# Q's last 64 contraction rows as two 64-row array tiles in an attention kernel

## The chip, the cores and the metric

The kernel runs on one core of one Trainium2 chip. The metric is device microseconds (us) of one execution. A kernel is timed in several runs and its median is quoted. Engines are named as in the profile: PE is TensorE's matmul, PEld its weight load (which normally overlaps PE), DVE is VectorE, ACT is ScalarE, POOL is GpSimd, SPq is the queue that issues DMA.

## The reference

Two independent attention blocks, A and B, have the same shapes; their outputs are concatenated. All data is bf16.

```python
B, Sq, D = 16, 144, 448            # x: [B, Sq, D]
H, Sk, Dh = 16, 512, 256           # k_cache, v_cache: [B, H, Sk, Dh]
q = (x @ wq).reshape(B, Sq, H, Dh).transpose(0, 2, 1, 3)
scores = einsum("bhqd,bhkd->bhqk", q, k_cache) * Dh ** -0.5
p = softmax(scores)
o = einsum("bhqk,bhkd->bhqd", p, v_cache)
out = o.transpose(0, 2, 1, 3).reshape(B, Sq, H * Dh) @ wo
```

What matters: Q contracts over D = 448 = 3 x 128 + 64, so the last of its four chunks fills only half of the 128 rows of TensorE's array.

## The kernel before

A unit is one head of one batch; there are 512. For each unit the kernel computes Q (transposed, 256 rows in two halves `dc` of 128), the scores S against K, exp, PV, and the output projection OP. Q is computed either for one batch (80 groups, 144 columns a matmul) or, in most of the kernel, for one head of a pair of batches (216 groups, 288 columns a matmul). The last 64 rows of Wq sit on partitions 64 to 127 of chunk 3, and partitions 0 to 63 of that chunk are set to zero once. So every matmul uses all 128 rows.

```python
wq_sb = sb("wq_sb", [128, 4, H * DH], BF16)
qp_ps = ps("qp_ps", [128, 2, 512], F32)            # two PSUM banks
# ... (cut)
def e2(v):
    return v.memset(wq_sb[0:64, 3, :], 0.0)        # zero rows of the last chunk
# ... (cut) Wq arrives by groups of four heads:
q.dma_start(wq_sb[:, 0:3, cols], w[0:384, cols].rearrange("(c p) n -> p c n", p=128))
q.dma_start(wq_sb[64:128, 3, cols], w[384:448, cols])
# ... (cut)
def t_q(U):                                        # n = 1 or 2 batches
    def e(t):
        for dc in range(2):
            for kc in range(4):
                c0 = h * DH + dc * 128
                acc = qp_ps[:, dc, 0:2 * SQ] if n == 2 else qp_ps[:, 0, dc * SQ:(dc + 1) * SQ]
                ins = t.matmul(acc, lhsT=wq_sb[:, kc, c0:c0 + 128],
                               rhs=xt_sb[:, kc, xo:xe + 1:max(xe - xo, 1), :], start=(kc == 0), stop=(kc == 3))
        return ins
```

A helper builds the order of the instructions on each engine; DVE copies the result of each group out of PSUM (`qt_sb<-qp_ps`).

## Time and profile before

| | before |
|---|---|
| median of the first 3 runs | 1057.1 us (1055.59 to 1058.32) |
| span of the profiled run | 1055.3 us |
| PE busy | 1031.0 us, 98% |
| DVE / ACT / POOL busy | 70% / 75% / 60% |
| Q groups | 80 of one batch, 216 of two |

The first part of the profile's page gives the busy time of each engine, its share of the span, and its instructions; the fourth part, the shares of the chain of waits that ended last:

```profile
PE 1031.0 (98%) x12376; PEld 875.0 (83%) x12376; DVE 740.9 (70%) x2039; ACT 793.9 (75%) x2365; POOL 636.6 (60%) x1030
...
PE 91%; DMA 5%; ACT 1%; DVE 1%; SPq 1%; issue 0%; POOL 0%; ACTq 0%; DVEq 0%
```

PE is the bottleneck. A busy PE need not stream at its best rate, so the next view matters more. This is the timeline of PE from 397 us: start in us, duration, engine, line, operation, output and inputs, rows and columns of the weights (`128*128`), the shape of the input, and how many matmuls the line merges.

```profile
397.78 0.54 PE L1259 MATMUL op_ps<-wo_sb,ring 128*128 128x448 bf16 x2
398.16 1.14 PE L1052 MATMUL qp_ps<-xt_sb,wq_sb 128*128 128x288 bf16 x8
399.14 0.66 PE L1086 MATMUL s_ps<-qt_sb,kt_sb 128*128 128x144 bf16 x8
399.64 0.66 PE L1142 MATMUL ot_ps<-pt_sb,v_sb 128*128 128x144 bf16 x8
400.14 0.54 PE L1259 MATMUL op_ps<-wo_sb,ring 128*128 128x448 bf16 x2
```

Read the starts, not the durations (one matmul's recorded duration overlaps the next). The eight matmuls of a pair's Q group take 399.14 - 398.16 = 0.98 us, 122.5 ns each for 288 columns; eight of 144 columns take 0.50 us, 62.5 ns each. The difference is 60 ns for 144 columns, so a column costs 0.417 ns and each matmul about 2.5 ns more. There is nothing between the groups: in this stretch PE streams columns without a gap, and as long as it does, only fewer columns can make it faster.

What PE waited for, in us in total, times, and the longest:

```profile
PE s_ps L1000 <- DMA v_sb<-in_A_k_cache_dram: 6.3, 4, 4.7
PE qp_ps L1052 <- DMA wq_sb<-in_B_wq_dram: 3.6, 1, 3.6
PE s_ps L1086 <- DMA kt_sb<-in_B_k_cache_dram: 2.9, 1, 2.9
PE qp_ps L1052 <- DMA xt_sb<-in_A_x_dram: 2.3, 1, 2.3
```

### The profile page before, as it was taken

What the parts mean: (1) busy time and instruction counts of PE and PEld (TensorE: products, weight loads), DVE (VectorE), ACT (ScalarE), POOL (GpSimd) and SP (SyncE); (2) the same over time, 40 slices, a digit from 0 to 9 for tenths busy, and PEclk for the clock granted to TensorE, in tenths of its full rate; (3) what the DMA queues carried; (4) which work ended last, traced back from release to release, by engine and by line L of the source; (5) the groups of instructions that cost most, each with busy time, mean ns of one, the idle gap of its engine ahead of it and who ended that gap; (6) DMA issues with size and microseconds to landing.
All of it is one profiled execution on the core that took longest, in us unless ns stands there. A gap on an engine that the chain in (4) does not pass through costs nothing.

```text
span 1055.3 us, 32320 instructions
## 1 busy us (share of the span) xinstructions
PE 1031.0 (98%) x12376; PEld 875.0 (83%) x12376; DVE 740.9 (70%) x2039; ACT 793.9 (75%) x2365; POOL 636.6 (60%) x1030
## 2 busy tenths in 40 slices
PE   6999999999999999999999899999999999999997
PEld 6999888888888888888878788888888888888885
DVE  4776666776766777777868667677776667777775
ACT  4887667777777777878857667777877777788785
POOL 3554556656666566666746556566666666666673
PEclk9999999999999999999999999999999999999999
DMA  9999999999999999999999999999999999999960
GB/s 316 372 343 291 294 291 248 283 299 271 264 305 260 248 286 262 304 289 280 283 281 343 279 283 287 303 284 292 251 279 280 278 286 298 296 254 274 292 201 14
DMA packets 589060, 294.15 MB, mean 279 GB/s; under 512 B 500832, under 2 KB 513632, under 8 KB 588896
## 3 DMA queue, kind: packets, MB, share of 16 engines
q1 hardware_dynamic: 588896, 291.99, 110.9%
q8 instruction: 99, 1.62, 0.6%
q14 instruction: 65, 0.53, 0.2%
HBM read 161.48 MB, written 4.13 MB: 157 GB/s over the span
## 4 chain that ended last, share of the span: by engine, by line
PE 91%; DMA 5%; ACT 1%; DVE 1%; SPq 1%; issue 0%; POOL 0%; ACTq 0%; DVEq 0%
PE s_ps L1086 23%; PE ot_ps L1142 23%; PE qp_ps L1052 22%; PE op_ps L1259 19%; DMA kt_sb<-in_B_k_cache_dram 2%; DMA v_sb<-in_A_k_cache_dram 2%; PE ot_ps L1158 2%; PE s_ps L1000 1%; PE qp_ps L1000 1%; DMA wq_sb<-in_B_wq_dram 1%; PE qp_ps L1259 1%; ACT rinv_sb L1179 0%; ACT pt_sb L1096 0%; DVE ring L1194 0%; DVE qt_sb L1066 0%
## 5 line engine op out<-in xcount | busy, mean ns | idle before, releaser
L1106 POOL TENSOR_TENSOR pp_sb<-pt_sb 128x288 f32<-128x288 bf16 x512 | 384.9, 752 | 322.5 <-ACT pt_sb L1096 308.1
L1096 ACT ACTIVATE pt_sb<-s_ps 128x288 bf16<-128x288 f32 x1024 | 364.6, 408 | 184.4 <-PE s_ps L1086 177.6
L1194 DVE TENSOR_TENSOR ring<-ot_ps,rinv_sb 128x288 bf16<-128x288 f32 (+2 forms) x640 | 241.9, 394 | 150.3 <-ACT rinv_sb L1179 145.8
L1086 PE MATMUL s_ps<-qt_sb,kt_sb 128*128 128x144 bf16 x4096 | 341.3, 226 | 4.7 <-DMA kt_sb<-in_B_k_cache_dram 2.9
L1142 PE MATMUL ot_ps<-pt_sb,v_sb 128*128 128x144 bf16 x4096 | 340.3, 226 | 0.0
L1086 PEld LDWEIGHTS s_ps<-qt_sb,kt_sb 128*128 128x128 bf16 x4096 | 287.7, 98 | 56.9 <-DVE qt_sb L1066 5.6
L1179 ACT ACTIVATE rinv_sb<-ln_sb 64x144 f32<-64x144 f32 x928 | 298.3, 321 | 24.3
L1052 PE MATMUL qp_ps<-xt_sb,wq_sb 128*128 128x288 bf16 (+1 forms) x2368 | 302.3, 271 | 6.6 <-DMA wq_sb<-in_B_wq_dram 3.6
L1259 PE MATMUL op_ps<-wo_sb,ring 128*128 128x448 bf16 x1120 | 285.2, 353 | 0.0
L1052 PEld LDWEIGHTS qp_ps<-xt_sb,wq_sb 128*128 128x128 bf16 x2368 | 212.3, 98 | 81.9 <-issue 7.5
L1142 PEld LDWEIGHTS ot_ps<-pt_sb,v_sb 128*128 128x128 bf16 x4096 | 274.5, 98 | 0.5
L1111 POOL TENSOR_TENSOR p_sb<-pp_sb 128x144 f32<-128x144 f32 x464 | 227.5, 490 | 74.6 <-DVE ps_sb L1120 10.4
L1209 DVE TENSOR_REDUCE run_sb<-ot_ps 128x1 bf16<-128x144 f32 x560 | 146.5, 304 | 79.4 <-ACT ln_sb L1166 44.3
L1120 DVE TENSOR_TENSOR ps_sb<-p_sb 64x144 bf16<-64x144 f32 x464 | 158.7, 342 | 44.4 <-POOL p_sb L1111 30.3
L1066 DVE CAST qt_sb<-qp_ps 128x576 bf16<-128x576 f32 x216 | 162.1, 751 | 21.3 <-PE qp_ps L1052 17.7
L1259 PEld LDWEIGHTS op_ps<-wo_sb,ring 128*128 128x128 bf16 x1120 | 94.0, 98 | 21.2
L1166 ACT ACTIVATE ln_sb<-ot_ps 128x144 f32<-128x144 f32 x232 | 67.9, 293 | 32.6 <-PE ot_ps L1158 25.3
L1158 PE MATMUL ot_ps<-ps_sb,ones 128*128 128x144 bf16 x280 | 63.4, 226 | 0.0
L1065 DVE CAST qt_sb<-qp_ps 128x288 bf16<-128x288 f32 x80 | 35.9, 448 | 4.8 <-PE qp_ps L1052 4.3
L1008 ACT ACTIVATE kt_sb<-qp_ps 128x512 bf16<-128x512 bf16 x48 | 28.9, 603 | 7.3 <-PE qp_ps L1000 7.3
L1111 POOL TENSOR_TENSOR ps_sb<-pp_sb 128x144 bf16<-128x144 f32 x48 | 23.5, 490 | 6.9 <-PE ot_ps L1158 0.3
L1158 PEld LDWEIGHTS ot_ps<-ps_sb,ones 128*128 128x128 bf16 x280 | 27.5, 98 | 0.0
(29 smaller groups left out, 153.4 us busy)
## 6 DMA issues: line engine op xcount, KB each, us to landing
v_sb<-in_A_v_cache_dram SPq DMA_DIRECT2D x128, 512.0 KB, 7.1
v_sb<-in_B_v_cache_dram SPq DMA_DIRECT2D x128, 512.0 KB, 7.5
v_sb<-in_A_k_cache_dram SPq DMA_DIRECT2D x24, 512.0 KB, 9.6
out_dram<-ost_sb SPq DMA_DIRECT2D x36, 112.0 KB, 6.2
wo_sb<-in_A_wo_dram SPq DMA_DIRECT2D x8, 448.0 KB, 8.7
wo_sb<-in_B_wo_dram SPq DMA_DIRECT2D x8, 448.0 KB, 9.0
wq_sb<-in_A_wq_dram SPq DMA_DIRECT2D x4, 768.0 KB, 10.1
wq_sb<-in_B_wq_dram SPq DMA_DIRECT2D x4, 768.0 KB, 10.6
```

What stands on the lines that cost most here:

```text
L1052: ins = t.matmul(acc, lhsT=wq_sb[:, kc, c0:c0 + 128], rhs=xt_sb[:, kc, xo:xe + 1:max(xe - xo, 1), :], start=(kc == 0), stop=(kc == 3))
L1066: return v.tensor_copy(qt_sb[:, a:b + 1:b - a, :, :], qp_ps[:, :, 0:2 * SQ].rearrange("p e (u q) -> p u e q", u=2))
L1086: ins = t.matmul(s_ps[bank][:, (c % 2) * SQ:(c % 2 + 1) * SQ], lhsT=kt_sb[:, 2 * c + dc, ko:ko + 128], rhs=qt_sb[:, qsl, dc, :], start=(dc ...
L1096: return a.activation(pt_sb[:, psl, 2 * k:2 * k + 2, :].rearrange("p b q -> p (b q)"), s_ps[bank][:, 0:2 * SQ], AF.Exp, scale=DH ** -0.5)
L1106: return g.tensor_tensor(pp_sb[:, :, :], pt_sb[:, psl, 0:2, :], pt_sb[:, psl, 2:4, :], op=ALU.add)
L1111: return g.tensor_tensor(dst, pp_sb[:, 0, :], pp_sb[:, 1, :], op=ALU.add)
L1120: return v.tensor_tensor(ps_sb[p0:p0 + 64, sl, :], p2_sb[0:64, :], p2_sb[64:128, :], op=ALU.add)
L1142: ins = t.matmul(ot_ps[ob][:, dc * SQ:(dc + 1) * SQ], lhsT=v_sb[:, vsl, j, c * DH + dc * 128:c * DH + (dc + 1) * 128], rhs=pt_sb[:, sl, c, ...
L1179: return a.activation(rinv_sb[p0:p0 + 64, sl, :], ln_sb[h0:h0 + 64, :], AF.Exp, scale=-1.0)
L1194: ins = v.tensor_tensor(ring[:, 2 * h:2 * h + 2, r0:r0 + q1 - q0], ot_ps[ob][:, 0:2 * SQ].rearrange("p (c q) -> p c q", c=2)[:, :, q0:q1], ...
L1209: return v.tensor_reduce(run_sb[:, k, j:j + 1], ot_ps[ob][:, 2 * SQ:3 * SQ], axis=AX.X, op=op)
L1259: ins = t.matmul(acc[0:m, 0:D], lhsT=ring[:, c, col0:col0 + m], rhs=wo_sb[:, c, :], start=(c == first), stop=(c == last))
```

## The change

The intent: in a pair group the two half-empty matmuls (one for each `dc`) should share one stream. Wq's last rows are packed so that the 64 rows for `dc` = 0 lie on partitions 0 to 63 and those for `dc` = 1 on 64 to 127. DVE copies x's last 64 rows to partitions 0 to 63 as well. Then two matmuls of 64 rows each run on the upper and the lower half of the array, into different PSUM banks, side by side. Single batches have one bank only; they use one 288-column matmul over all 128 rows whose x is padded with zeros, in place of two of 144 columns.

```diff
-        wq_sb = sb("wq_sb", [128, 4, H * DH], BF16)
+        wq_sb = sb("wq_sb", [128, 3, H * DH], BF16)
+        wr_sb = sb("wr_sb", [128, H * 128], BF16)
+        xz_sb = sb("xz_sb", [128, 2, 2, SQ], BF16)
 ...
-                return q.dma_start(wq_sb[64:128, 3, cols], w[384:448, cols]).then_inc(sems["wq%d" % hg], 16)
+                last = w[384:448, cols].rearrange("k (h e m) -> k h e m", e=2, m=128)
+                dst = wr_sb[:, hg * 512:(hg + 1) * 512].rearrange("p (h m) -> p h m", m=128)
+                q.dma_start(dst[0:64], last[:, :, 0, :]).then_inc(sems["wq%d" % hg], 16)
+                return q.dma_start(dst[64:128], last[:, :, 1, :]).then_inc(sems["wq%d" % hg], 16)
 ...
+                    return v.tensor_copy(xt_sb[0:64, 3, gx, :], xt_sb[64:128, 3, gx, :])   # pairs, once per batch
 ...
-                for dc in range(2):
-                    for kc in range(4):
+                wr = wr_sb[:, h * 128:(h + 1) * 128]
+                if n == 1:
+                    t.matmul(qp_ps[:, 0, 0:2 * SQ], lhsT=wr, rhs=xz_sb[:, z, :, :], start=True, stop=False,
+                             skip_group_check=True)
+                for kc in range(3):
+                    for dc in range(2):
                         c0 = h * DH + dc * 128
 ...
+                if n == 2:
+                    for dc in range(2):
+                        p = slice(64 * dc, 64 * dc + 64)
+                        ins = t.matmul(qp_ps[:, dc, 0:2 * SQ], lhsT=wr[p], rhs=xt_sb[p, 3, xs_, :],
+                                       start=False, stop=True)
 ...
+            for u in of_step(lq, i + 1):          # the copies, one unit ahead of their use
+                if q_pair(u):
+                    t_q_rest(u)
```

More of the change, by code (lines that the diff above doesn't have):

```diff
@@ L905, in e2 @@
             def e2(v):
-                return v.memset(wq_sb[0:64, 3, :], 0.0)
-            S.add(DVE, e2, writes=[("wqz", 0)], name="wqz")
+                v.memset(xz_sb[64:128, :, 0, :], 0.0)
+                return v.memset(xz_sb[0:64, :, 1, :], 0.0)
+            S.add(DVE, e2, writes=[("xzz", 0)], name="xzz")
             def e4(g):
@@ L924, in e @@
                     sems["wq%d" % hg], 16)
-                return q.dma_start(wq_sb[64:128, 3, cols], w[384:448, cols]).then_inc(sems["wq%d" % hg], 16)
-            S.add(SP, e, writes=[(("wq", hg), pr)], dma_sem="wq%d" % hg, n_dma=2, name="wq%d.%d" % (pr, hg))
+                last = w[384:448, cols].rearrange("k (h e m) -> k h e m", e=2, m=128)
+                dst = wr_sb[:, hg * 512:(hg + 1) * 512].rearrange("p (h m) -> p h m", m=128)
+                q.dma_start(dst[0:64], last[:, :, 0, :]).then_inc(sems["wq%d" % hg], 16)
+                return q.dma_start(dst[64:128], last[:, :, 1, :]).then_inc(sems["wq%d" % hg], 16)
+            S.add(SP, e, writes=[(("wq", hg), pr)], dma_sem="wq%d" % hg, n_dma=3, name="wq%d.%d" % (pr, hg))
         def t_load_wo(pr, wg):
@@ L1037, in bass_concat_heads__mha_block_cached__gqa_block_cached__near_ridge_kernel, with t_xr, e, e0 @@
                 q_slot[u] = q_live[u] = sl
+        def t_xr(g, n):
+            gx = g % NX
+            if n == 2:
+                def e(v):
+                    return v.tensor_copy(xt_sb[0:64, 3, gx, :], xt_sb[64:128, 3, gx, :])
+                S.add(DVE, e, reads=[(("xt", gx), g)], writes=[(("xr", gx), g)], name="xr%d" % g)
+                return
+            z = g % 2
+            def e0(v):
+                return v.tensor_copy(xz_sb[0:64, z, 0, :], xt_sb[64:128, 3, gx, :])
+            def e1(v):
+                return v.tensor_copy(xz_sb[64:128, z, 1, :], xt_sb[64:128, 3, gx, :])
+            for k, e in ((0, e0), (1, e1)):
+                S.add(DVE, e, reads=[(("xt", gx), g), ("xzz", 0)], writes=[(("xz", z), g)], name="xz%d.%d" % (g, k))
+        xr_made = set()
+        def t_q_rest(U):
+            pr = unit(U)[0]
+            n = q_pair(U)
+            for u in q_units(U):
+                g = pr * Bn + (u - pr * NU) // H
+                if (g, n) not in xr_made:
+                    xr_made.add((g, n))
+                    t_xr(g, n)
         def t_q(U):
@@ L1044, in t_q @@
             hg = h // 4
+            z = gs[0] % 2
+            rest = [(("xz", z), gs[0])] if n == 1 else [(("xr", g % NX), g) for g in gs]
             def e(t):
                 ins = None
-                for dc in range(2):
-                    for kc in range(4):
+                xs_ = slice(xo, xe + 1, max(xe - xo, 1))
+                wr = wr_sb[:, h * 128:(h + 1) * 128]
[4 more added lines that the diff above has]
+                    for dc in range(2):
                         c0 = h * DH + dc * 128
                         acc = qp_ps[:, dc, 0:2 * SQ] if n == 2 else qp_ps[:, 0, dc * SQ:(dc + 1) * SQ]
-                        ins = t.matmul(acc, lhsT=wq_sb[:, kc, c0:c0 + 128],
-                                       rhs=xt_sb[:, kc, xo:xe + 1:max(xe - xo, 1), :], start=(kc == 0), stop=(kc == 3))
+                        ins = t.matmul(acc, lhsT=wq_sb[:, kc, c0:c0 + 128], rhs=xt_sb[:, kc, xs_, :],
+                                       start=(n == 2 and kc == 0), stop=(n == 1 and kc == 2),
+                                       skip_group_check=(n == 1))
+                if n == 2:
+                    for dc in range(2):
+                        p = slice(64 * dc, 64 * dc + 64)
+                        ins = t.matmul(qp_ps[:, dc, 0:2 * SQ], lhsT=wr[p], rhs=xt_sb[p, 3, xs_, :],
+                                       start=False, stop=True)
                 return ins
-            S.add(PE, e, reads=[(("wq", hg), pr), ("wqz", 0)] + [(("xt", g % NX), g) for g in gs],
+            S.add(PE, e, reads=[(("wq", hg), pr)] + [(("xt", g % NX), g) for g in gs] + rest,
                   writes=[(bk, ("q", U)) for bk in q_banks[:n]], banks=q_banks[:n], name="Q%d" % U)
@@ L1391, in bass_concat_heads__mha_block_cached__gqa_block_cached__near_ridge_kernel @@
                 t_tr(u, 0)
+            for u in of_step(lq, i + 1):
+                if q_pair(u):
+                    t_q_rest(u)
             for u in of_step(lq, i):
                 if q_pair(u):
+                    t_q_rest(u)
                     t_q(u)
```

## The prediction

> **What bounds it.** TensorE. The profile's first part gives PE 1031.0 of 1055.3 us (98%), the chain of waits is 91% PE, and the stretch view shows PE busy 199.8 of 200 us from 300 to 500 us, at clock 1.00. The timeline shows it streaming: eight 144-column matmuls take 0.50 us (62.5 ns each), eight of 288 take 0.98 us (122.5 ns each): 0.417 ns a column plus about 2.5 ns a matmul. DVE (70%), ACT (75%) and POOL (60%) have room. The DMA queue mostly waits for PE to free slots (its own waits: 306 us in one row); PE waits for DMA in a few places only (6.3, 3.6, 2.9, 2.3 us).
>
> **What changes.** Single batches (80 of 296 Q groups): eight 144-column matmuls become one of 288 and six of 144, the same columns: 80 x 2.5 ns = 0.2 us. Pairs (216 groups, the 1728 matmuls of 288 columns in the groups view): six full matmuls stay, the two zero-padded ones become two 64-row tiles, on different rows and PSUM banks. If they run side by side, one stream goes: 122.5 ns x 216 = 26.5 us, all on the critical path. That is the ceiling: 1057 - 26 = 1031 us, 2.5%.
>
> **What it costs.** Each pair group changes the array's tiling twice, 432 changes. The Trainium skill (TensorEngine Tiling (Array Packing), Key Properties) says that changing tiling mode, not just tile, drains the TensorE. No trace here shows one: every matmul of before is 128 by 128. Break-even is 122.5 / 2 = 61 ns a change. An estimate from the page TensorE: Matmul & The Clock Gate (Part 2): the wavefront needs about 128 array cycles, 53 ns at 2.4 GHz, to leave, and the next weight load may no longer hide behind the matmul ahead (recorded as 98 ns, normally overlapped). So 50 to 80 ns a change if only the wavefront is exposed, 150 or more if the load's latency is too. I expect most or all of the gain to be given back: net -60 to +150 ns a pair group, -13 to +32 us; my middle is a small loss.
>
> Side costs: some 45 to 70 DVE copies of 64x144 bf16, perhaps 0.15 us each (estimate; DVE's 128x512 copy took 0.415 us): about 10 us on an engine 30% idle, one step ahead, off the path. Wq's last rows arrive in two DMAs of 256-byte pieces instead of one of 2 KB pieces; the Wq wait (3.6 us at 522 us) and the first Q (8.7 us, now behind two copies) may grow by 1 to 3 us together.
>
> **Time.** 1060 us, 1033 to 1105 eight times in ten. Faster by over 2%: 0.14 (needs changes under about 10 ns each); within 2%: 0.51; slower by over 2%: 0.35.
>
> **What would show it.** In the timeline, from the start of a pair's Q group to the following S matmul: 0.98 us before; 0.86 if tiling changes are free; over 0.98 if they cost over 61 ns each. The two tile matmuls should start within tens of ns of each other; 122 ns apart means no overlap and no saving. The gaps before the first tile matmul and before the first S matmul after give the two drains apart. PE's waits for DVE's copies should be near zero after the first batch.
>
> **What would make it wrong.** Nearly free tiling changes (1031 to 1036); a full pipeline latency at each change, about 230 ns as the records show for one matmul (about 1130); DMA that cannot follow a faster PE around 520 to 610 us, where K transposes already hold PE up.

## The result, and the profile after

The changed kernel takes 1075.65 us (median of 4 runs, 1074.76 to 1076.54), before 1056.34 us beside it. The ratio is 1.0176, 95% interval 1.0157 to 1.0195: 1.8% slower. (Ratios are the mean time of one kernel's runs over that of the other's of the same rounds, so not quite the ratio of the medians quoted.)

The same views of the changed kernel: busy times and shares of the chain of waits,

```profile
PE 1050.2 (98%) x12296; PEld 833.4 (78%) x12296; DVE 752.0 (70%) x2083; ACT 794.3 (74%) x2365; POOL 630.9 (59%) x1030
...
PE 91%; ACT 3%; DMA 3%; DVE 2%; issue 1%; SPq 0%; ACTq 0%; DVEq 0%
```

and PE's timeline around one pair group:

```profile
400.76 0.54 PE L1306 MATMUL op_ps<-wo_sb,ring 128*128 128x448 bf16 x2
401.14 0.90 PE L1093 MATMUL qp_ps<-xt_sb,wq_sb 128*128 128x288 bf16 x6
401.97 0.30 PE L1099 MATMUL qp_ps<-xt_sb,wr_sb 64*128 64x288 bf16 x2
402.20 0.67 PE L1133 MATMUL s_ps<-qt_sb,kt_sb 128*128 128x144 bf16 x8
402.71 0.66 PE L1189 MATMUL ot_ps<-pt_sb,v_sb 128*128 128x144 bf16 x8
```

The group takes 402.20 - 401.14 = 1.06 us instead of 0.98. PE's busy share is 98% as before, so the busy time does not show what happened; the starts do. Six full matmuls should take 6 x 122.5 = 735 ns, but the first tile starts 0.83 us after the group. Here are the starts of the single matmuls and weight loads of this group, in ns from the span's start (read from the trace's records):

```
401751  matmul, 128 rows, 288 columns (the sixth)
401965  weight load, 64 rows
401969  weight load, 64 rows
401970  matmul, 64 rows, 288 columns   (219 ns after the sixth; 122.5 without a gap)
401973  matmul, 64 rows, 288 columns   (3 ns later: side by side)
402195  weight load, 128 rows (S)
402199  matmul, 128 rows, 144 columns  (226 ns after the second tile; 122.5 without a gap)
402272  matmul, 128 rows, 144 columns  (73 ns later; 62.5 in the stream)
```

The tiles do run side by side. But PE has a gap of about 96 ns on the way into the tiles and about 103 ns on the way out, and the second matmul after it comes 10 ns late. The view of what the weight loads waited for shows the same in one row, for all 216 groups:

```profile
PEld qp_ps L1099 <- issue: 51.5, 216, 0.5
PEld qp_ps L1093 <- DVE xt_sb L1049: 6.1, 11, 0.8
```

"issue" means that the engine waited for nothing the profile can name: no semaphore, no other engine. The tiles' loads sit idle 51.5 / 216 = 0.24 us each time. That is more than PE's gap of 96 ns because the load also loses its lead. Before, a load started one matmul ahead of its own; here it starts about 92 ns after the sixth matmul's last column should have streamed (401751 + 122.5), 4 or 5 ns ahead of its own matmul. This short lead alone does not name the cause: in the kernel before, loads of S that wait for `qt_sb` also start 4 or 5 ns ahead.

The sums over all starts of the two profiled runs, in us (a gap is a start-to-start distance less the columns' time; "waits" are gaps over 25 ns elsewhere, whatever their cause):

| | before | after |
|---|---|---|
| streaming (columns, and 2.5 ns a matmul) | 1020.4 | 993.7 |
| 216 gaps into the tiles | 0 | 20.7 |
| 216 gaps out of them, and the late second matmul | 0 | 22.3 + 2.3 |
| second tile of the pair | 0 | 0.7 |
| waits | 23.7 | 22.8 |
| before the first start, after the last, rest | 11.3 | 11.0 |
| span | 1055.3 | 1073.6 |

The stream saved 26.7 us, as forecast. The changes of tiling took 46.0 us, the second tile's 0.7 included: 213 ns a group, 106 ns a change. Not all of the row "waits" is waiting: 4.9 us of it before and 4.3 after are matmuls that follow each other at up to twice the usual distance, in the first 12 us and just after long waits. In the kernel before, after the 3.6 us wait for B's Wq, 144-column matmuls start 120 ns apart instead of 62.5, and the view of stretches gives a granted clock of 0.83 from 530 to 540 us. What PE waited for, after:

```profile
PE s_ps L1006 <- DMA v_sb<-in_A_k_cache_dram: 4.5, 1, 4.5
PE qp_ps L1093 <- DMA wr_sb<-in_B_wq_dram: 4.1, 1, 4.1
PE qp_ps L1087 <- DVE xz_sb L1058: 3.8, 3, 2.8
PE qp_ps L1087 <- DVE qt_sb L1112: 1.9, 2, 1.0
...
PE qp_ps L1093 <- DVE xt_sb L1049: 0.8, 2, 0.5
PE s_ps L1133 <- DMA kt_sb<-in_B_k_cache_dram: 0.4, 1, 0.4
```

Waits for DVE's copies (`xz_sb`, `xt_sb`) at the first matmul of Q groups are new. At all Q groups' first matmuls the gaps over 25 ns sum to 13.5 us against 7.2 before.

### The profile page after: what moved, and what is told of

Read it like the earlier page. It is cut to its first block, busy times and chain, and to the rows that moved or that the text cites. A ratio compares the mean times of both kernels' runs of the same rounds, so it can differ in the third digit from the quotient of the medians.

```text
span 1073.7 us, 32198 instructions
## 1 busy us (share of the span) xinstructions
PE 1050.2 (98%) x12296; PEld 833.4 (78%) x12296; DVE 752.0 (70%) x2083; ACT 794.3 (74%) x2365; POOL 630.9 (59%) x1030
## 4 chain that ended last, share of the span: by engine, by line
PE 91%; ACT 3%; DMA 3%; DVE 2%; issue 1%; SPq 0%; ACTq 0%; DVEq 0%
PE s_ps L1133 24%; PE ot_ps L1189 22%; PE op_ps L1306 18%; PE qp_ps L1093 17%; PE qp_ps L1099 4%; DMA kt_sb<-in_B_k_cache_dram 2%; ACT rinv_sb L1226 2%; PE ot_ps L1205 2%; PE qp_ps L1087 1%; ACT pt_sb L1143 1%; PE s_ps L1006 1%; PE qp_ps L1006 1%; DVE ring L1241 1%; DMA wr_sb<-in_B_wq_dram 1%; PE qp_ps L1306 1%
## 5 line engine op out<-in xcount | busy, mean ns | idle before, releaser
L1153 POOL TENSOR_TENSOR pp_sb<-pt_sb 128x288 f32<-128x288 bf16 x512 | 379.8, 742 | 347.0 <-ACT pt_sb L1143 334.1
L1241 DVE TENSOR_TENSOR ring<-ot_ps,rinv_sb 128x288 bf16<-128x288 f32 (+2 forms) x640 | 242.0, 395 | 156.8 <-ACT rinv_sb L1226 154.5
L1133 PEld LDWEIGHTS s_ps<-qt_sb,kt_sb 128*128 128x128 bf16 x4096 | 271.0, 98 | 69.9 <-DVE qt_sb L1112 3.0
L1093 PE MATMUL qp_ps<-xt_sb,wq_sb 128*128 128x288 bf16 (+1 forms) x1776 | 239.1, 271 | 5.6 <-DMA wr_sb<-in_B_wq_dram 4.1
L1093 PEld LDWEIGHTS qp_ps<-xt_sb,wq_sb 128*128 128x128 bf16 x1776 | 161.9, 98 | 71.4 <-DVE xt_sb L1049 6.1
L1099 PE MATMUL qp_ps<-xt_sb,wr_sb 64*128 64x288 bf16 x432 | 64.1, 293 | 0.0
L1099 PEld LDWEIGHTS qp_ps<-xt_sb,wr_sb 64*128 64x128 bf16 x432 | 20.7, 93 | 51.5 <-issue 51.5
```

The costliest lines, as they stand in the source:

```text
L1093: ins = t.matmul(acc, lhsT=wq_sb[:, kc, c0:c0 + 128], rhs=xt_sb[:, kc, xs_, :], start=(n == 2 and kc == 0), stop=(n == 1 and kc == 2), ski ...
L1133: ins = t.matmul(s_ps[bank][:, (c % 2) * SQ:(c % 2 + 1) * SQ], lhsT=kt_sb[:, 2 * c + dc, ko:ko + 128], rhs=qt_sb[:, qsl, dc, :], start=(dc ...
L1153: return g.tensor_tensor(pp_sb[:, :, :], pt_sb[:, psl, 0:2, :], pt_sb[:, psl, 2:4, :], op=ALU.add)
L1241: ins = v.tensor_tensor(ring[:, 2 * h:2 * h + 2, r0:r0 + q1 - q0], ot_ps[ob][:, 0:2 * SQ].rearrange("p (c q) -> p c q", c=2)[:, :, q0:q1], ...
```

## The experiments

Theory: at each change of tiling no column streams for about 100 ns, two changes a group (the expectations say "empty array"; whether the array is empty then, the records do not show). Rivals: (A) the side costs, (B) a 64-row weight load that cannot hide, whatever changes, (C) a wait for a PSUM bank, (D) the second tile, (E) the use of two tiles rather than 64 rows as such. The kernels ran in three sets, each beside the kernel before, whose medians were 1055.54, 1056.32 and 1054.52 us.

### All rows: everything but the tiling

```diff
-                        p = slice(64 * dc, 64 * dc + 64)
+                        p = slice(0, 128)
```

> Everything of the change but the tiling: the last two matmuls of a pair group use all 128 rows (same packed weights, same copied x; the result is wrong on purpose). No tiling change is left. Theory (each tiling change costs about 100 ns of empty array): back to the time of before, 1054 to 1060 us, a pair group 0.98 us. Rival A (the side costs: DVE copies, 256-byte DMA pieces, alternating PSUM banks): stays at 1066 to 1076 us.

1061.78 us, ratio 1.0052 (1.0027 to 1.0077). The pair group is back at 0.98 us:

```profile
403.31 0.90 PE L1093 MATMUL qp_ps<-xt_sb,wq_sb 128*128 128x288 bf16 x6
404.05 0.41 PE L1099 MATMUL qp_ps<-xt_sb,wr_sb 128*128 128x288 bf16 x2
404.29 0.66 PE L1133 MATMUL s_ps<-qt_sb,kt_sb 128*128 128x144 bf16 x8
```

The row of 51.5 us of "issue" is gone. So the tiling is most of the loss, about 13 of 19 us (19.3 and 6.2 us, each against the kernel before beside it). But the run missed its range: some 6 us of side costs remain, so rival A holds in part, and the last experiment below looks for them. (The comparison with the reference called this result correct although Q is wrong on purpose; at these inputs it does not notice an error in the last 64 of 448 rows. So that the changed kernel passed says nothing about those rows either.)

### Four tiles at the end, or two in the middle and two at the end

Both use four 144-column tiles, a batch at a time. The second kernel only moves the first two up.

```diff
+                def tiles(u, stop):
+                    g = xo + u * (xe - xo)
+                    for dc in range(2):
+                        p = slice(64 * dc, 64 * dc + 64)
+                        i = t.matmul(qp_ps[:, dc, u * SQ:(u + 1) * SQ], lhsT=wr[p], rhs=xt_sb[p, 3, g, :],
+                                     start=False, stop=stop, skip_group_check=True)
+                    return i
 # at the end:           after the loop over kc: tiles(0, True); ins = tiles(1, True)
 # in the middle as well: after kc == 0: tiles(0, True); after the loop: ins = tiles(1, True)
```

> The two 288-column tiles become four 144-column tiles, batch by batch, all at the end of the group: still two tiling changes, but each tile loads weights twice, the second time while its own matmul is in flight. Theory: 1075 to 1079 us (2.5 ns more a group). Rival B (a 64-row weight load can never hide behind a matmul on its own rows; tiling changes as such are cheap): one more exposed load of about 95 ns a group, about 1096 us.

1074.06 us, ratio 1.0175 (1.0147 to 1.0203): the same as the change, a microsecond below the stated range. The loads of the second two tiles start about 11 ns after the first two matmuls, on the same rows, and the next matmul on these rows starts 73 ns after the first where its columns take 62.5. So a 64-row load does hide behind a matmul on its own rows but for 10 ns, and rival B falls.

> The same four 144-column tiles, but the first two are moved up behind the first two full matmuls of the group: four tiling changes a group instead of two, same columns, same loads as the run with all four at the end. Theory: 211 ns more a group than after, x 216 = 46 us: about 1121 us (1115 to 1127). Rival B: same time as the run with all four at the end.

1115.89 us, ratio 1.0571 (1.0544 to 1.0598): 41.8 us more than its neighbour, for 432 more changes, 97 ns of wall time each. The timeline of one group shows four gaps where there were two:

```profile
403.17 0.41 PE L1101 MATMUL qp_ps<-xt_sb,wq_sb 128*128 128x288 bf16 x2
403.51 0.24 PE L1094 MATMUL qp_ps<-xt_sb,wr_sb 64*128 64x144 bf16 x2
403.68 0.66 PE L1101 MATMUL qp_ps<-xt_sb,wq_sb 128*128 128x288 bf16 x4
404.27 0.24 PE L1094 MATMUL qp_ps<-xt_sb,wr_sb 64*128 64x144 bf16 x2
404.44 0.67 PE L1140 MATMUL s_ps<-qt_sb,kt_sb 128*128 128x144 bf16 x8
```

Two full matmuls should take 245 ns and take 0.34 us; a 144-column tile pair should take about 65 and takes 0.17. The row of idle weight loads doubles, from this in the kernel with all four at the end

```profile
PEld qp_ps L1094 <- issue: 51.2, 216, 0.2
```

to this:

```profile
PEld qp_ps L1094 <- issue: 102.5, 432, 0.2
```

The gaps of the trace are again 96 ns in and 103 ns out, with tiles half as long. The loss goes with the number of changes, not with columns or loads.

### The tiles first

The tile pair moves ahead of the six full matmuls (`start=True` on the tiles, `False` on the rest).

```diff
+                if n == 2:
+                    for dc in range(2):
+                        p = slice(64 * dc, 64 * dc + 64)
+                        t.matmul(qp_ps[:, dc, 0:2 * SQ], lhsT=wr[p], rhs=xt_sb[p, 3, xs_, :],
+                                 start=True, stop=False)
                 for kc in range(3):
```

> The tile pair moves from the end of the group to its start, where the matmuls ahead write other PSUM banks. Still two tiling changes. Theory: no difference, 1073 to 1078 us, entry gap about 95 ns, exit gap about 105 to 115 ns. Rival C (the entry gap is a wait for the full matmul that still writes the tile's PSUM bank): the entry gap goes, 97 ns x 216 = 21 us, about 1055 us.

1074.93 us, ratio 1.017 (1.014 to 1.0201). In most groups (199 of 216) an OP matmul of 448 columns is ahead now, in another bank:

```profile
399.94 0.54 PE L1306 MATMUL op_ps<-wo_sb,ring 128*128 128x448 bf16 x2
400.42 0.30 PE L1092 MATMUL qp_ps<-xt_sb,wr_sb 64*128 64x288 bf16 x2
400.65 0.91 PE L1098 MATMUL qp_ps<-xt_sb,wq_sb 128*128 128x288 bf16 x6
```

Its successor starts a median 285 ns later, where such a matmul's successor in the stream starts after 189: again 96 ns. Rival C falls, and the gap depends neither on the length of the matmul ahead (288 or 448 columns) nor on its bank.

### One tile only

```diff
-                    for dc in range(2):
+                    for dc in range(1):
                         p = slice(64 * dc, 64 * dc + 64)
```

(and `stop` set on the last full matmul of the other bank; the result is wrong).

> Only the first tile of the pair is left, the second is dropped (wrong result on purpose). Still two tiling changes. Theory (the tiles overlap fully, all the loss is in the changes): same as after, 1073 to 1077 us. Rival D (the second tile costs time of its own, as a stream or a load): up to 122.5 ns less a group, down to 1049 us.

1072.07 us, ratio 1.0145 (1.0119 to 1.0171), 1 us below the theory's range and far from what rival D allows. The gaps in and out sum to 20.7 and 22.3 us, as with two tiles; the second tile itself costs 0.7 us in the sums. So it is nearly free. The other 3 us or so against the changed kernel beside it (1076.03) are not traced to one place, and may be noise: the intervals of the two ratios (1.0119 to 1.0171 and 1.0158 to 1.02) overlap.

### 64 rows on one tile, in the kernel before

```diff
-                for dc in range(2):
-                    for kc in range(4):
+                # pairs: kc outside, dc inside, so that both 64-row matmuls come last
+                        p = slice(64, 128) if n == 2 and kc == 3 else slice(0, 128)
-                        ins = t.matmul(acc, lhsT=wq_sb[:, kc, c0:c0 + 128], ...
+                        ins = t.matmul(acc, lhsT=wq_sb[p, kc, c0:c0 + 128], ...
```

> The kernel before, with the zero rows of the last chunk left out of the pair groups: its last two matmuls take rows 64 to 127 only, both on the same tile, one after the other (right result, no copies, DMA as before). Two tiling changes a group, nothing saved. Theory: 211 ns x 216 = 46 us over before, 1098 to 1104 us. Rival E (64 rows alone cost nothing; only the use of two tiles does): 1054 to 1058 us.

1091.52 us, ratio 1.0319 (1.0293 to 1.0346). Rival E falls: leaving out rows that hold zeros costs 35 us. The group takes 1.18 us instead of 0.98 (the view merges its eight matmuls under the form of the first):

```profile
403.25 1.25 PE L1054 MATMUL qp_ps<-xt_sb,wq_sb 128*128 128x288 bf16 x8
404.43 0.67 PE L1088 MATMUL s_ps<-qt_sb,kt_sb 128*128 128x144 bf16 x8
```

With the run of one tile above, this shows that a single 64-row matmul among full ones is already a change of tiling. The gaps sum to 20.7 us in, 20.0 out and 2.3 for the late second matmul, and another 2.3 between the two tile matmuls (133 ns apart instead of 122.5): 45.3 us, as forecast. But the time missed the stated range by 7 us, because PE's waits elsewhere fell from 23.7 to 14.6 us by the sums (2.7 of the 14.6 are matmuls on the slower clock, against 4.9). The waits that are left at the first matmul of Q groups are, for instance:

```profile
PE qp_ps L1054 <- DMA xt_sb<-in_A_x_dram: 2.8, 1, 2.8
PE qp_ps L1054 <- DMA wq_sb<-in_B_wq_dram: 2.0, 1, 2.0
PE qp_ps L1054 <- DVE qt_sb L1067: 0.6, 1, 0.6
```

(before, 3.6 for B's Wq; and the row of 2.9 for B's K has gone from the view). My theory left out that part of a loss on PE can be taken out of its waits. That a slower PE gives the DMA more time is the likely reason, but no run tests it alone.

### The copies earlier

```diff
-            for u in of_step(lq, i + 1):
+            for u in of_step(lq, i + 1) + [v for v in of_step(lq, i + 6) if v >= P0]:
```

(`P0` is where single batches give way to pairs.) The changed kernel ran again beside it.

> The change, with DVE's copies of x for the pair groups put 6 units ahead of their use instead of 1. Tiling as in the change. In the run with full rows PE's waits at the first matmul of Q groups summed to 14.3 us against 7.2 before, about 4 us of it at twelve first pair groups. Theory: those waits go, 3 to 5 us less than after: 1071 to 1073 us. Rival (they do not matter, or only move): as after, 1075 to 1076 us.

> The changed kernel again, for the comparison with early copies on the same chip: 1073 to 1077 us.

Early copies: 1071.87 us, ratio 1.0134 (1.0114 to 1.0155). The changed kernel: 1076.03 us, ratio 1.0179 (1.0158 to 1.02). The row of weight loads that wait for these copies (`PEld qp_ps L1093 <- DVE xt_sb L1049: 6.1` us above) is gone. The profiled run of this kernel was its slowest (1074.89), so its page is not read for the sum.

To see whether the two costs simply add, the same move was made in the kernel with all rows, with that kernel beside it:

> No tiling change (the last two matmuls of a pair group use all 128 rows, result wrong on purpose) and the copies 6 units ahead. Theory (the 6 us that the full-rows run kept over before are mostly PE's waits for late copies): 3 to 5 us less than the full-rows run beside it, 1056 to 1059 us, within 2 or 3 us of before. Rival (they come from the 256-byte DMA pieces or the order of the matmuls): stays at 1061 to 1063 us.

> The full-rows run again, beside the one with early copies: 1060 to 1063 us.

1057.01 us, ratio 1.0025 (1.0009 to 1.0041), beside 1060.99 us, ratio 1.0062 (1.0044 to 1.0079). So about 4 of the 6 us go when the copies come earlier, with or without tiles. (In the profiled runs of these two all-rows kernels PE's waits fell from 28.4 to 23.6 us, 2.1 of it at the slower clock after long waits.) The remaining 2 to 3 us are the rest of the change; the copies for single batches and the Wq DMA of 256-byte pieces are candidates (the Wq wait was 4.3 us in the second all-rows run, 3.6 before), but PE's gap at that place was 4.2 us in one run of the changed kernel and 1.8 in the other, so this is left open. What the weight loads of the all-rows kernel waited for, before the move:

```profile
PEld qp_ps L1093 <- DVE xt_sb L1049: 6.1, 11, 0.8
PEld qp_ps L1087 <- DVE xz_sb L1058: 5.2, 3, 3.4
```

and after it, where the first row has no counterpart:

```profile
PEld qp_ps L1087 <- DVE xz_sb L1058: 3.1, 1, 3.1
```

No version beat the kernel before. An estimate of the next step: two heads in one stay in the tiles would save 2 x 122.5 = 245 ns against 213, so 32 ns x 108 = 3.5 us. It needs two more PSUM banks, and all eight that the kernel allocates are in use (two for Q, three for S, two for PV, one for OP), so it was not built.

## Why the prediction was right or wrong

The time, 1075.65 us, lies in the stated range (1033 to 1105) and in the class given the best chance (within 2%), but it is well above the middle, 1060.

- "If they run side by side, one stream goes: 122.5 ns x 216 = 26.5 us, all on the critical path." Right: streaming fell by 26.7 us, and the tiles start 3 ns apart.
- "Changing tiling mode (not just tile) drains the TensorE" (the Trainium skill, TensorEngine Tiling (Array Packing), Key Properties), on which the prediction's cost rests. The trace agrees that a change costs PE time, and the runs with zero, two and four changes a group put a number to it: 96 ns in, 103 ns out and about 10 ns on the matmul after. The drain itself is not in the records, since ends are modelled: the sixth matmul's stands 67 ns after the first tile's start.
- "50 to 80 ns a change if only the wavefront is exposed, 150 or more if the load's latency is too ... my middle is a small loss." The mechanism was right, the size was off. This is the term that failed: 106 ns a change, between the two cases. The net is 213 - 122.5 = 90 ns a group, within the stated -60 to +150, but 19 us over 216 groups and not the 3 us of my middle. I had taken the wavefront's 53 ns (an estimate from TensorE: Matmul & The Clock Gate, Part 2) as most of a change; the measured gap is about twice that. What fills the other half, no run here separates, nor whether the gap is a drain or a load that is not allowed ahead: the load's record starts only at the end of the gap.
- "Off the path" for the copies, and 1 to 3 us of side costs. Wrong: the side costs are 6 us (all rows against before), of which about 4 go when the copies come earlier. DVE had 30% idle, but a copy stands in line behind DVE's other work: in the second all-rows run each one but those that follow another copy starts 30 to 32 ns after an operation of L1241 ends, and that line's operations themselves wait for ACT (116.5 us in one row of the changed kernel). Put one unit ahead, the copy is ready late. Six units ahead, it is not: the first pair copy then starts at 102.3 us instead of 114.8.
- Not foreseen: PE's waits, slower clock included, shrank in the kernels where PE was slower: 29.1 us with all rows, 22.8 in the change, 17.1 with four changes a group. Between the all-rows kernel and the change the tiling should cost 46.0 - 26.5 = 19.5 us by the sums, and cost about 13, because the waits fell by 6.3. This partly hid both misses. That the whole loss, 19.3 us, is so near those 19.5 is luck: the side costs of 6 us and the fall of the waits cancel.

## What to carry to other kernels

Count changes of tiling before counting columns: here one stay in 64-row tiles costs about 213 ns of PE, so it has to save more than about 500 columns of stream (an estimate, 213 / 0.417) before it gains anything, and zero-padding to 128 rows was the better choice for 288. Read such losses from the start-to-start distances and from the "issue" row of the weight loads, since PE's busy share (98% in both kernels) does not show them. And a helper operation on an engine with idle time is off the critical path only if it is issued far enough ahead in that engine's order.

## What the Trainium skill lacked or had wrong

- TensorEngine Tiling (Array Packing), Key Properties, says that a mode switch drains the TensorE but gives no cost, and its section Performance Considerations recommends row tiling for contract dimensions up to 64 without it: 96 ns in and 103 ns out, plus 10 ns on the second matmul; the way in is the same after 288 and after 448 columns.
- No page says that one 64-row matmul among 128-row ones already pays this: 96 ns in and 103 ns out with one tile only. Two matmuls on the same tile paid 96 ns in and 92.5 ns out, 35 us for 216 groups in wall time.
- TensorE: Matmul & The Clock Gate, Part 3, lists that a weight load overlaps matmuls in flight only when the row group differs. Within a stay in the tiles, the reload of the same rows hid but for 10 ns (73 ns start to start for 62.5 ns of columns), which agrees with Part 2 of the same page (loads into the background buffer). Part 3's start distance of about 4 ns between tiles agrees: 3 ns.
- The same page, Back-to-back issue gap, gives about 81 ns a matmul for N = 128 with a weight load each. Here 144 columns with new weights each took 62.5 ns, and the 128-column transposes a median 56 ns; the formula that the page calls that of the isolated matmul (N / 2.4 + 2.5) fits this kernel's stream (189 ns at 448 columns, too) outside the stretches on the slower clock.
